# Attention scores of two heads in blocks of 32 queries, four blocks side by side in the PSUM partitions, in one run of TensorE

## The chip, the cores and the metric

The kernel runs on one core of one Trainium2 chip. The metric is the device time of one execution in microseconds (us); the median of several runs counts.

A core has five engines with an instruction queue each: TensorE (matrix multiplies, PE in the profile, its weight loads PEld), VectorE (DVE), ScalarE (ACT), GpSimd (POOL) and SyncE (SP), which here issues every DMA. TensorE writes to PSUM, eight banks of 512 float32 columns in 128 partitions; VectorE and ScalarE read it, GpSimd and DMAs can't.

## What is computed

An attention of two parts feeds a mixing layer and a feed-forward net. `B, H, S, D` are 8, 8, 576 and 64; everything is float32.

```python
q_d, k_d, v_d = means over groups of 4 positions            # 144 positions
out_up = repeat(softmax(scale * q_d @ k_d.T) @ v_d, 4)      # pooled attention
mask = abs(pos[:, None] - pos[None, :]) < 4                 # 7 keys for each query
scores = where(mask, scale * q @ k.T, -1e9)
out_local = softmax(scores) @ v                             # local attention
x = (out_up + out_local)  as (batch, 576, 512)              # heads side by side
h = x.T @ U @ V                                             # mixes positions, rank 32
u = x + h.T
out = u + relu(u @ w_ch1) @ w_ch2                           # 512 -> 2048 -> 512
```

## The kernel before

**Work.** Two heads make a pair (`b`, `hp`), so there are 32. Head 0 of a pair lies in partitions 0 to 63, head 1 in 64 to 127 (`heads`). The first five pairs (`NE`) take another way (`local_blocks`); the other 27, the late pairs, are those of this change. The feed-forward (`ffn1`, `ffn2`) takes 256 steps over 8 batches, two halves of 288 positions and 16 blocks of 128 hidden units; a step is 12 matmuls into `ps_h` and 12 into four banks `acc`. Each weight and each input of it is a pair of a high and a low part in a reduced float32 form (`W1H`, `W1L`, `uH`, `uL`, ...), of which three products are taken.

**A late pair** goes this way:

- SyncE loads `gq` and `gT`, the transposed q and (padded) k of both heads, 128 partitions by 576 and 582. GpSimd makes the pooled `smq` and `smk` of them (L407, L410).
- Dense scores (`qk_group`, L658): 96 queries against the 102 keys around them, six blocks a head; of a block's scores only the band of 7 a query is wanted later. A first run takes four blocks of both heads into two banks (4 x 102 = 408 columns), a second the other two blocks and, behind them in the same banks, the pooled scores (L671, 72 x 144, two a head).
- ScalarE copies the dense scores out of PSUM (`se`, L676), and SyncE writes them to a scratch in HBM, `s_s` (L680), at a row pitch of 103 with rows written at a pitch of 102. So the read back (`sc`, L686) with the pitch of 103 finds the 7 wanted scores of a query at the start of its row.
- The pooled scores go through maximum (DVE L473), exponential (ACT L481), transposes (PE L495) and a second product (PE L506) to `od`, and by HBM (`up_s`) to the local part.
- The local part (`local_attn`): softmax of `sc`, then GpSimd multiplies (L727) and VectorE sums (L732) windows of v; the result goes by HBM (`x_s`) to `mix_part`, which makes `uH` and `uL` for the feed-forward.

**What sets the order.** `Plan` simulates five engines with a duration given for each operation (`op(PE, 1.6, ...)`) and priorities (attention before feed-forward, `FILL`), and writes each engine's instructions in the resulting order. On the chip each engine works its list in that order, and waits on semaphores. The attention of batch b + 1 is spread among the feed-forward steps of batch b. Of the PSUM banks, two (`ps_m`, tag `m`) serve all small work of the late pairs: dense and pooled scores (both banks at once, `psum_pair`), `ps_t`, `ps_a`, `ps_hu` and `ps_u` one each.

Of the kernel before, what the change touches and what calls it, by code (L numbers as in the profile page):

```python
# [11 lines left out]
F32 = mybir.dt.float32  # L12
# [3 lines left out]
AF = mybir.ActivationFunctionType  # L16
# [5 lines left out]
PE, DVE, ACT, POOL, SP = range(5)  # L22
# [31 lines left out]
class Plan:  # L54
# [6 lines left out]
    def buf(self, pool, shape, dt, name, tag=None, bufs=1):  # L61
        return Buf(self, pool, shape, dt, name, tag or name, bufs)

    def op(self, eng, dur, fn, r=(), w=(), prio=0.0, after=(), lat=None, move=0.0, at=0.0):
        o = Op()
        o.eng, o.dur, o.fn, o.prio, o.succ, o.ndep, o.ready = eng, dur, fn, prio, [], 0, at
        o.lat, o.move = LATENCY[eng] + SLACK * (SLACK_FROM <= prio < 1000) if lat is None else lat, move
        deps = set(after)
        bufs = []
        for k in r:  # L70
            b = k[0] if isinstance(k, tuple) else k
            bufs.append(b)
            if k in self.last_w:
                deps.add(self.last_w[k])
            self.readers.setdefault(k, []).append(o)
        for k in w:
            b = k[0] if isinstance(k, tuple) else k
            bufs.append(b)
            if k in self.last_w:
                deps.add(self.last_w[k])  # L80
            deps.update(self.readers.get(k, ()))
            self.readers[k] = []
            self.last_w[k] = o
        deps.discard(o)
        o.margin = MARGIN[eng] * (MARGIN_FROM <= prio < 1000 and any(d.eng != eng for d in deps))
        o.bufs = [b for b in dict.fromkeys(bufs) if isinstance(b, Buf)]
        for b in o.bufs:
            b.uses += 1
        for d in deps:
            d.succ.append(o)  # L90
        o.ndep = len(deps)
        self.ops.append(o)
        return o
# [108 lines left out]
def attn_mix_ffn_kernel(ctx: ExitStack, tc, q, kp, vp, qT, kT, v, U, Ub, V, w1, w2, mask, band, eye, sel, pool, vw, ident, outT):  # L202
    nc = tc.nc
    B, H, S, D = q.shape
# [3 lines left out]
    SD = S // 4  # L208
    QH = SD // 2
# [18 lines left out]
    NB = 6  # L228
    HB = NB // 2
    QB = S // NB  # L230
    KB = band.shape[1] // (HB + 1)

    plan = Plan()
    op, buf = plan.op, plan.buf

    const = ctx.enter_context(tc.tile_pool(name="const", bufs=1))
    loc = ctx.enter_context(tc.tile_pool(name="loc", bufs=1))
# [3 lines left out]
    dram = ctx.enter_context(tc.tile_pool(name="dram", bufs=1, space=bass.MemoryType.DRAM))  # L241
    ps_acc = ctx.enter_context(tc.tile_pool(name="ps_acc", bufs=1, space=bass.MemoryType.PSUM))
    ps_h = ctx.enter_context(tc.tile_pool(name="ps_h", bufs=2, space=bass.MemoryType.PSUM))
    ps_m = ctx.enter_context(tc.tile_pool(name="ps_m", bufs=2, space=bass.MemoryType.PSUM))

    def psum(pool, name, tag, bufs):
        return buf(pool, [128, 512], F32, name, tag, bufs)

    def psum_pair(pool, name, tag, bufs):
        two = [psum(pool, name, tag, bufs) for _ in range(2)]  # L250
        for t in two:
            t.mates = two
        return two

    def dma(fn, r, w, prio, kb=295.0, issue=0.47, lat=1.3):
        late = (3.0 if r else 4.0) * (prio >= 50)
        return op(SP, issue, fn, r, w, prio, move=0.01 + kb / 290.0, at=AT if prio >= 35 else 0.0, lat=lat + late)
# [4 lines left out]
    def act(n, fn, r, w, prio, base=0.143):  # L262
        return op(ACT, n / 1200.0 + base, fn, r, w, prio)
# [127 lines left out]
    def work(is_early, pool, shape, dt, name, tag=None, bufs=1):  # L391
        if is_early:
            return buf(early_pool, shape, dt, name, tag, 2)
        return buf(pool, shape, dt, name, tag, bufs)

    heads = [slice(hh * D, (hh + 1) * D) for hh in range(2)]
    count = {"b": 0}

    def global_attn(b, hp, up_s, prio, qt=None, kt=None, vb=None):
        e = qt is not None  # L400
        h0 = 2 * hp
        sq = work(e, glo, [128, SD], F32, "smq")
        sk = work(e, glo, [128, SD], F32, "smk")
# [9 lines left out]
        if e:  # L413
            qr, kr = qt, kt
        else:
            qr = buf(glo, [128, S], F32, "gq")
            kr = buf(glo, [128, SPAD], F32, "gT")
# [20 lines left out]
        else:  # L438
            vr = [work(e, glo, [QH, 2, 4, D], F32, "vr") for _ in range(2)]
            for hh in range(2):  # L440
                dma(lambda hh=hh: nc.sync.dma_start(
                    out=vr[hh](), in_=v[b, h0 + hh].rearrange("(a p r) d -> p a r d", a=2, r=4)),
# [3 lines left out]
            for hh in range(2):  # L446
                x = vr[hh]
                pool_tt(256, lambda x=x: nc.gpsimd.tensor_tensor(  # L448
                    out=x()[:, :, 0:2, :], in0=x()[:, :, 0:2, :], in1=x()[:, :, 2:4, :], op=ALU.add), [x], [x], prio)
                pool_tt(128, lambda x=x, vs=vss[hh]: nc.gpsimd.tensor_tensor(  # L450
                    out=vs(), in0=x()[:, :, 0, :], in1=x()[:, :, 1, :], op=ALU.add), [x], [vss[hh]], prio)
        view = lambda t, n: t()[:QH, :2 * n].rearrange("p (a k) -> p a k", a=2)
        rs = work(e, glo, [QH, 2, 2], F32, "rs", bufs=2)
        if e:
            ps = psum_pair(ps_m, "ps_s", "m:g", 2)
            scores = lambda t: view(t, SD)

            def s_mm():
                for a in range(2):
                    for hh, o in enumerate(heads):  # L460
                        nc.tensor.matmul(view(ps[hh], SD)[:, a], sq()[o, a * QH:(a + 1) * QH], sk()[o],
                                         start=True, stop=True)
            op(PE, pw(prio) * 1.4, s_mm, [sq, sk], ps, prio)
        else:
            s_s = buf(dram, [2, S, KB + 1], F32, "s_s", bufs=4)
            qk_group(0, NBA, qr, kr, s_s, prio - 0.5)
            ps = qk_group(NBA, NB, qr, kr, s_s, prio - 0.4, sq, sk)
            scores = lambda t: pooled_view(t)
        Es = []
        for hh in range(2):  # L470
            p = ps[hh]
            mx = work(e, glo, [QH, 2], F32, "mx", bufs=2)
            dve(288, lambda p=p, mx=mx: nc.vector.tensor_reduce(  # L473
                out=mx(), in_=scores(p), axis=AX.X, op=ALU.max), [p], [mx], prio)
# [14 lines left out]
        for hh in range(2):  # L489
# [13 lines left out]
            def a_mm(ET=ET, pa=pa, vs=vsx[hh]):  # L503
# [6 lines left out]
                out=od()[:QH, 2 * hh:2 * hh + 2, :], in0=view(pa, D),  # L510
# [141 lines left out]
            w = bass.AP(tensor=a.tensor, offset=a.offset, ap=[[NPOS * D, 64], [1, (NPOS + 6) * D]])  # L652
            nc.sync.dma_start(out=t[hh * 64:(hh + 1) * 64].rearrange("p s d -> p (s d)"), in_=w)

    NBA = 4
    pooled_view = lambda t: t()[:QH, (NB - NBA) * KB:(NB - NBA) * KB + 2 * SD].rearrange("p (a k) -> p a k", a=2)

    def qk_group(n0, n1, qr, kr, s_s, prio, sq=None, sk=None):  # L658
        m = n1 - n0
        view = lambda t: t()[:QB, :m * KB].rearrange("p (i k) -> p i k", i=m)  # L660
        ps = psum_pair(ps_m, "ps_b", "m:b" if sq is None else "m:g", 2)

        def mm():
            for n in range(n0, n1):
                for hh, o in enumerate(heads):
                    nc.tensor.matmul(view(ps[hh])[:, n - n0], qr()[o, n * QB:(n + 1) * QB],  # L666
                                     kr()[o, n * QB:n * QB + KB], start=(n == n0), stop=(n == n1 - 1 and sq is None))
            if sq is not None:
                for a in range(2):
                    for hh, o in enumerate(heads):  # L670
                        nc.tensor.matmul(pooled_view(ps[hh])[:, a], sq()[o, a * QH:(a + 1) * QH], sk()[o],  # L671
                                         start=False, stop=(a == 1))
        op(PE, 0.4 + 0.083 * 2 * m + (0.0 if sq is None else 0.5), mm, [qr, kr] + ([] if sq is None else [sq, sk]), ps, prio)
        for hh in range(2):
            se = buf(loc, [QB, m, KB], F32, f"se{m}", bufs=2)
            act(m * KB, lambda p=ps[hh], se=se: nc.scalar.activation(se(), view(p), AF.Copy), [ps[hh]], [se], prio)  # L676

            def put(hh=hh, se=se):
                dst = s_s()[hh].rearrange("(i p) k -> i (p k)", i=NB)[n0:n1, 0:QB * KB]
                nc.sync.dma_start(out=dst.rearrange("i (p k) -> p i k", k=KB), in_=se())  # L680
            dma(put, [se], [(s_s, n0, hh)], prio, 55 * m)
        return ps

    def local_scores(s_s, prio):
        sc = buf(loc, [128, NPOS, 7], F32, "sc")
        dma(lambda: nc.sync.dma_start(out=sc(), in_=s_s()[:, :, 0:7].rearrange("h (c s) o -> (h c) s o", s=NPOS)),  # L686
            [(s_s, n0, hh) for n0 in (0, NBA) for hh in range(2)], [sc], prio, 315, lat=0.8)
        return sc

    def local_attn(b, hp, up_s, x_s, s_s, prio):  # L690
        h0 = 2 * hp
        lb = lambda shape, name, tag=None, bufs=1: buf(loc, shape, F32, name, tag, bufs)
        vl = lb([128, NPOS + 6, D], "vl")
        sc = local_scores(s_s, prio - 1.5)
        dma(lambda: load_padded(vl(), vp, b, h0), [], [vl], prio + 0.1, 500, 1.2, 2.1)
        ms, mx = lb([128, NPOS, 7], "ms"), lb([128, NPOS], "lmx")
# [203 lines left out]
    for i in range(len(steps) + LAG):  # L900
        if i < len(steps):
            b, t, fc = steps[i]
# [69 lines left out]
```

## Time and profile before

| | |
|---|---|
| median of 3 runs | 1083.02 us (1081.96 to 1083.38) |
| the profiled execution | 1082.04 us |
| its span, first to last instruction | 1080.0 us |
| mean granted clock of TensorE | 0.979 |
| TensorE busy | 1044.0 us (97%) |
| VectorE, ScalarE, GpSimd busy | 537.1, 412.7, 559.2 us |
| late pairs' dense matmuls (L666) | 648 records, 44.1 us |
| late pairs' pooled matmuls (L671) | 216 records, 18.4 us |

A row of a group of instructions names line, engine, operation and tiles (out<-in), partitions x elements, count, then busy time, mean ns of one, and what ended the idle time before it. A row of the timeline has start, length, engine, line, operation and tiles, and how many records it merges. A matmul's row lasts until its modelled end, so neighbouring rows overlap; what counts is the distance from start to start. A wait "<- issue" is time in which nothing was released that the profile shows.

### The profile page before, as it was taken

How to read it: one execution, taken by the hardware profiler on the slowest of the kernel's cores; microseconds unless marked ns; L12 is line 12 of the kernel's file. 1: busy time of each engine (PE TensorE's matmuls, PEld its weight loads, DVE VectorE, ACT ScalarE, POOL GpSimd, SP SyncE). 2: the span in 40 equal slices, each digit the busy share in tenths (PEclk: the TensorE clock that was granted, in tenths of full speed). 3: DMA queues.
4: the chain of work that ended last, by engine and by line, in shares of the span. 5: the costliest groups of instructions: out<-in, count | busy, mean ns of one | idle time of the engine just before them, and what ended most of it. 6: DMA issues, size and time to landing. Idle time of an engine off the chain costs nothing.

```text
span 1080.0 us, 22707 instructions
## 1 busy us (share of the span) xinstructions
PE 1044.0 (97%) x8696; PEld 1012.8 (94%) x8696; DVE 537.1 (50%) x1093; ACT 412.7 (38%) x1374; POOL 559.2 (52%) x580
## 2 busy tenths in 40 slices
PE   7798998998999999999999999999999999999998
PEld 6677897997999999999999999999999999999998
DVE  5888898554554445545454534533466343212111
ACT  4787554343334433333444324422444222211110
POOL 3754567587475756566566726753666614201010
PEclk8897999998999999999999999999999999999999
DMA  6635864555556555554756345642666231000000
GB/s 195 188 118 158 222 195 112 147 121 141 121 142 137 133 147 126 130 137 110 158 139 156 89 97 140 161 104 61 154 148 169 64 71 47 23 1 23 2 22 22
DMA packets 222972, 125.00 MB, mean 116 GB/s; under 512 B 170449, under 2 KB 201491, under 8 KB 222865
## 3 DMA queue, kind: packets, MB, share of 16 engines
q1 hardware_dynamic: 222864, 123.57, 45.5%
q8 instruction: 68, 1.11, 0.4%
q14 instruction: 40, 0.32, 0.1%
HBM read 85.18 MB, written 38.35 MB: 114 GB/s over the span
## 4 chain that ended last, share of the span: by engine, by line
PE 86%; DVE 7%; DMA 2%; ACT 2%; POOL 1%; issue 1%; SPq 0%; DVEq 0%; POOLq 0%; ACTq 0%
PE acc L837 36%; PE ps_h L814 36%; PE ps_b L666 3%; PE ps_a L506 3%; PE ps_hu L774 2%; DVE c L333 1%; DVE c L335 1%; PE ps_t L495 1%; PE ps_b L671 1%; DVE c L328 1%; PE ps_u L789 1%; DMA s_s<-se 1%; DMA xL<-x_s 1%; PE ps_ba L598 1%; DMA kd<-in_kT 0%
## 5 line engine op out<-in xcount | busy, mean ns | idle before, releaser
L837 PE MATMUL acc<-hH,W2H 128*128 128x288 f32 x1024 | 313.2, 306 | 0.0
L814 PE MATMUL ps_h<-uH,W1H 128*128 128x288 f32 x1024 | 307.1, 300 | 0.3 <-ACT ob L608 0.3
L814 PE MATMUL ps_h<-uL,W1H 128*128 128x288 f32 x1024 | 304.8, 298 | 0.0
L814 PE MATMUL ps_h<-uH,W1L 128*128 128x288 f32 x1024 | 304.7, 298 | 0.0
L837 PE MATMUL acc<-hH,W2L 128*128 128x288 f32 x1024 | 302.9, 296 | 0.6 <-POOL W2L L340 0.6
L837 PE MATMUL acc<-hL,W2H 128*128 128x288 f32 x1024 | 303.2, 296 | 0.0
L822 DVE SCALAR_TENSOR_TENSOR hL<-ps_h,hH 128x288 fp32r<-128x288 f32 x256 | 116.6, 456 | 374.8 <-ACT hH L821 373.5
L727 POOL TENSOR_TENSOR Pt<-vl,at 128x896 f32<-128x896 f32 (+1 forms) x135 | 230.9, 1787 | 104.4 <-DVE acc L732 50.6
L821 ACT ACTIVATE hH<-ps_h 128x288 fp32r<-128x288 f32 x256 | 105.0, 410 | 454.3 <-PE ps_h L814 452.8
L837 PEld LDWEIGHTS acc<-hH,W2H 128*128 128x128 f32 x1024 | 193.2, 189 | 6.2 <-issue 3.8
L814 PEld LDWEIGHTS ps_h<-uH,W1H 128*128 128x128 f32 x1024 | 194.2, 190 | 1.9 <-issue 1.2
L814 PEld LDWEIGHTS ps_h<-uL,W1H 128*128 128x128 f32 x1024 | 194.3, 190 | 0.0
L837 PEld LDWEIGHTS acc<-hH,W2L 128*128 128x128 f32 x1024 | 193.2, 189 | 0.8 <-POOL W2L L340 0.8
L814 PEld LDWEIGHTS ps_h<-uH,W1L 128*128 128x128 f32 x1024 | 193.7, 189 | 0.0
L837 PEld LDWEIGHTS acc<-hL,W2H 128*128 128x128 f32 x1024 | 193.5, 189 | 0.0
L732 DVE TENSOR_REDUCE acc<-Pt 128x128 f32<-128x1024 f32 (+1 forms) x135 | 144.8, 1104 | 9.5 <-POOL Pt L727 3.6
L797 POOL TENSOR_TENSOR uL<-xT,uH 128x288 fp32r<-128x288 f32 x56 | 44.0, 807 | 103.4 <-ACT uH L795 103.4
L766 POOL TENSOR_TENSOR xL<-xL,xH 116x640 fp32r<-116x640 f32 x28 | 44.3, 1580 | 82.7 <-ACT xH L765 61.3
L847 POOL TENSOR_TENSOR o<-uH,uL 128x288 f32<-128x288 f32 x64 | 50.1, 814 | 53.3 <-DMA out_t<-o 53.3
L721 ACT ACTIVATE Pt<-ul 128x128 f32<-128x128 f32 (+1 forms) x135 | 48.4, 443 | 24.9 <-DVE acc L732 24.6
L448 POOL TENSOR_TENSOR vr<-vr 72x256 f32<-72x256 f32 x54 | 41.6, 770 | 29.7 <-DMA vr<-in_v 29.5
L676 ACT ACTIVATE se<-ps_b 96x408 f32<-96x408 f32 (+1 forms) x108 | 40.8, 419 | 33.3 <-PE ps_b L666 15.7
(136 smaller groups left out, 1225.3 us busy)
## 6 DMA issues: line engine op xcount, KB each, us to landing
vl<-in_vp SPq DMA_DIRECT2D x54, 240.0 KB
out_t<-o SPq DMA_DIRECT2D x64, 144.0 KB
s_s<-se SPq DMA_DIRECT2D x54, 153.0 KB
w1r<-in_W SPq DMA_DIRECT2D x16, 512.0 KB
w2r<-in_W SPq DMA_DIRECT2D x16, 512.0 KB
Y<-x_s SPq DMA_DIRECT2D x112, 72.0 KB
xL<-x_s SPq DMA_DIRECT2D x28, 287.5 KB
gT<-in_kT SPq DMA_DIRECT2D x27, 291.0 KB
```

Of the source, the lines that this page charges most:

```text
L448: pool_tt(256, lambda x=x: nc.gpsimd.tensor_tensor(out=x()[:, :, 0:2, :], in0=x()[:, :, 0:2, :], in1=x()[:, :, 2:4, :], op=ALU.add), [x], ...
L676: act(m * KB, lambda p=ps[hh], se=se: nc.scalar.activation(se(), view(p), AF.Copy), [ps[hh]], [se], prio)
L721: act(n * D, lambda n=n, ps=ps, Pt=Pt: nc.scalar.activation(Pt()[:, :n, :, 7], ul()[:, ps, :], AF.Copy), [ul], [(Pt, 1)], prio, 0.16)
L727: nc.gpsimd.tensor_tensor(out=Pt()[:, :n, :, 0:7].rearrange("p s d o -> p o s d"), in0=win, in1=at()[:, ps, :].rearrange("p s o -> p o s") ...
L732: dve(8.5 * n * D, lambda n=n, ps=ps, Pt=Pt: nc.vector.tensor_reduce(out=acc()[:, ps, :], in_=Pt()[:, :n], axis=AX.X, op=ALU.add), [(Pt, 0 ...
L766: pool_tt(640, lambda: nc.gpsimd.tensor_tensor(out=xL(), in0=xL().bitcast(F32), in1=xH().bitcast(F32), op=ALU.subtract), [xL, xH], [xL], prio)
L797: pool_tt(TN, lambda uH=uH, uL=uL, uf=uf: nc.gpsimd.tensor_tensor(out=uL()[:, hp, :], in0=uf(), in1=uH()[:, hp, :].bitcast(F32), op=ALU.su ...
L814: nc.tensor.matmul(ps()[:, :TN], w[:, dc, fs], u()[:, dc, :], start=(n == 0), stop=(n == 3 * NDC - 1))
L821: last_h[i] = act(TN, lambda: nc.scalar.activation(hH(), ps()[:, :TN], AF.Relu), [ps], [hH], FIRST, 0.05)
L822: dve(TN, lambda: nc.vector.scalar_tensor_tensor(hL(), ps()[:, :TN], 0.0, hH().bitcast(F32), op0=ALU.max, op1=ALU.subtract), [ps, hH], [hL ...
L837: nc.tensor.matmul(ac[e]()[:, :TN], W2[w][:, fc, es], hx(), start=(fc == 0 and n == 0), stop=(fc == NFC - 1 and n == 2))
L847: pool_tt(TN, lambda e=e, o1=o1: nc.gpsimd.tensor_tensor(out=o1()[:, :TN], in0=uH()[:, e, :].bitcast(F32), in1=uL()[:, e, :].bitcast(F32), ...
```

## The change

Blocks have 32 queries and 38 keys (`QL`, `KL`), 18 a head. Block n goes to row `r = n // 4` and column `c = n % 4`: its 32 queries lie in the PSUM partitions 32c to 32c + 31, and its 38 scores in the columns from 38r on, so that four blocks lie side by side in the partitions and five rows take 190 columns (the fifth row holds two blocks). The pooled scores follow in the same bank, and dense and pooled matmuls are one operation of the plan, with one pair of banks. ScalarE copies four rows of 128 partitions and then the fifth of 64. SyncE writes four transfers a head instead of two, one for each 32 partitions. The scratch has a pitch of 39 instead of 103. Lines between the two places of the diff move up by one, those behind it down by 6: the feed-forward's L814 and L837 become L820 and L843, the dense matmuls L666 become L667.

```diff
-            s_s = buf(dram, [2, S, KB + 1], F32, "s_s", bufs=4)
-            qk_group(0, NBA, qr, kr, s_s, prio - 0.5)
-            ps = qk_group(NBA, NB, qr, kr, s_s, prio - 0.4, sq, sk)
+            s_s = buf(dram, [2, S, KL + 1], F32, "s_s", bufs=4)
+            ps = late_scores(qr, kr, sq, sk, s_s, prio - 0.4)
...
+    QL, KL = 32, 38
+    NL = S // QL
+    NR, NX = divmod(NL, 4)
+    pooled_view = lambda t: t()[:QH, (NR + 1) * KL:(NR + 1) * KL + 2 * SD].rearrange("p (a k) -> p a k", a=2)
+
+    def late_scores(qr, kr, sq, sk, s_s, prio):
+        view = lambda t: t()[:, :(NR + 1) * KL].rearrange("p (r k) -> p r k", r=NR + 1)
+        ps = psum_pair(ps_m, "ps_b", "m:g", 2)
 
         def mm():
-            for n in range(n0, n1):
+            for n in range(NL):
+                r, c = divmod(n, 4)
                 for hh, o in enumerate(heads):
-                    nc.tensor.matmul(view(ps[hh])[:, n - n0], qr()[o, n * QB:(n + 1) * QB],
-                                     kr()[o, n * QB:n * QB + KB], start=(n == n0), stop=(n == n1 - 1 and sq is None))
...
+                    nc.tensor.matmul(view(ps[hh])[c * QL:(c + 1) * QL, r], qr()[o, n * QL:(n + 1) * QL],
+                                     kr()[o, n * QL:n * QL + KL], start=(r == 0), stop=(c == 3 and n + 4 >= NL))
+            for a in range(2):
+                for hh, o in enumerate(heads):
+                    nc.tensor.matmul(pooled_view(ps[hh])[:, a], sq()[o, a * QH:(a + 1) * QH], sk()[o],
+                                     start=False, stop=(a == 1))
+        op(PE, 1.6, mm, [qr, kr, sq, sk], ps, prio)
         for hh in range(2):
-            se = buf(loc, [QB, m, KB], F32, f"se{m}", bufs=2)
-            act(m * KB, lambda p=ps[hh], se=se: nc.scalar.activation(se(), view(p), AF.Copy), [ps[hh]], [se], prio)
+            se = buf(loc, [128, NR + 1, KL], F32, "se", bufs=2)
+            parts = ((0, NR, 128), (NR, NR + 1, NX * QL))
+            for r0, r1, n in parts:
+                act((r1 - r0) * KL, lambda p=ps[hh], se=se, r0=r0, r1=r1, n=n: nc.scalar.activation(
+                    se()[:n, r0:r1], view(p)[:n, r0:r1], AF.Copy), [ps[hh]], [(se, r0)], prio)
 
             def put(hh=hh, se=se):
-                dst = s_s()[hh].rearrange("(i p) k -> i (p k)", i=NB)[n0:n1, 0:QB * KB]
-                nc.sync.dma_start(out=dst.rearrange("i (p k) -> p i k", k=KB), in_=se())
-            dma(put, [se], [(s_s, n0, hh)], prio, 55 * m)
+                for c in range(4):
+                    to = s_s()[hh, c * QL:(c + 1) * QL, :]
+                    n = NR + (c < NX)
+                    dst = bass.AP(tensor=to.tensor, offset=to.offset, ap=[[KL, QL], [4 * QL * (KL + 1), n], [1, KL]])
+                    nc.sync.dma_start(out=dst, in_=se()[c * QL:(c + 1) * QL, 0:n])
+            dma(put, [(se, 0), (se, NR)], [(s_s, hh)], prio, 100, 1.7)
```

The fourth late pair on TensorE, before: its first run (`ps_b` are the dense scores, `acc` and `ps_h` the feed-forward).

```order
L837 MATMUL acc_1554<-hL,W2H 128x288
L837 MATMUL acc_1554<-hH,W2L 128x288
L666 MATMUL ps_b<-gT,gq 96x102 x8
L837 MATMUL acc_1561<-hH,W2H 128x288
```

Its second run, some 20 rows later, with the pooled scores (`smk`, `smq`):

```order
L814 MATMUL ps_h<-uL,W1H 128x288
L814 MATMUL ps_h<-uH,W1L 128x288
L666 MATMUL ps_b<-gT,gq 96x102 x4
L671 MATMUL ps_b<-smk,smq 72x144 x4
L837 MATMUL acc_1554<-hH,W2H 128x288
```

And the same pair's only run now:

```order
L820 MATMUL ps_h<-uL,W1H 128x288
L820 MATMUL ps_h<-uH,W1L 128x288
L667 MATMUL ps_b<-gT,gq 32x38 x36
L671 MATMUL ps_b<-smk,smq 72x144 x4
L843 MATMUL acc_1615<-hH,W2H 128x288
```

The feed-forward is interrupted in one place instead of two, for 36 small dense matmuls instead of 8 and 4 larger ones; the four pooled ones stay.

SyncE's list around the same pair's scores, before (`gq`, `gT` are loads for the next pair, `ul` and `sc` reads from HBM for the local part):

```order
L680 DMA s_s<-se_2260 96x4x102
L680 DMA s_s<-se_2277 96x4x102
L526 DMA gq<-in_qT 128x576
L526 DMA gT<-in_kT 128x582
L680 DMA s_s<-se_2307 96x2x102
L680 DMA s_s<-se_2316 96x2x102
L715 DMA ul<-up_s 128x576
L686 DMA sc<-s_s 128x9x7
```

and now:

```order
L525 DMA gq<-in_qT 128x576
L525 DMA gT<-in_kT 128x582
L686 DMA s_s<-se 32x5x38 x2
L686 DMA s_s<-se 32x4x38 x2
L686 DMA s_s<-se 32x5x38 x2
L686 DMA s_s<-se 32x4x38 x2
L692 DMA sc<-s_s 128x9x7
```

Eight transfers of 32 partitions stand where two of four blocks and two of two blocks stood, all behind the loads for the next pair, and the read `sc` follows them at once.

More of the change, by code (lines that the diff above doesn't have):

```diff
@@ L653, in load_padded @@
             nc.sync.dma_start(out=t[hh * 64:(hh + 1) * 64].rearrange("p s d -> p (s d)"), in_=w)
[L655 to L661, printed above, removed]
+    QL, KL = 32, 38
+    NL = S // QL
@@ L668, in mm @@
[L668 to L673, printed above, removed]
-        for hh in range(2):
-            se = buf(loc, [QB, m, KB], F32, f"se{m}", bufs=2)
-            act(m * KB, lambda p=ps[hh], se=se: nc.scalar.activation(se(), view(p), AF.Copy), [ps[hh]], [se], prio)
-            def put(hh=hh, se=se):
-                dst = s_s()[hh].rearrange("(i p) k -> i (p k)", i=NB)[n0:n1, 0:QB * KB]
-                nc.sync.dma_start(out=dst.rearrange("i (p k) -> p i k", k=KB), in_=se())
-            dma(put, [se], [(s_s, n0, hh)], prio, 55 * m)
+                    nc.tensor.matmul(view(ps[hh])[c * QL:(c + 1) * QL, r], qr()[o, n * QL:(n + 1) * QL],
+                                     kr()[o, n * QL:n * QL + KL], start=(r == 0), stop=(c == 3 and n + 4 >= NL))
@@ L686, in local_scores @@
         dma(lambda: nc.sync.dma_start(out=sc(), in_=s_s()[:, :, 0:7].rearrange("h (c s) o -> (h c) s o", s=NPOS)),
-            [(s_s, n0, hh) for n0 in (0, NBA) for hh in range(2)], [sc], prio, 315, lat=0.8)
+            [(s_s, hh) for hh in range(2)], [sc], prio, 315, lat=0.8)
         return sc
```

## The prediction

> **What bounds the kernel now.** I read the page first (busy shares and the chain that ended last), then a table by stretch, then the chain and the waits of TensorE from 265 us on, and last the rows of TensorE around two runs of dense scores. From the page:
>
> ```profile
> span 1080.0 us, 22707 instructions
> PE 1044.0 (97%) x8696; PEld 1012.8 (94%) x8696; DVE 537.1 (50%) x1093; ACT 412.7 (38%) x1374; POOL 559.2 (52%) x580
> PE 86%; DVE 7%; DMA 2%; ACT 2%; POOL 1%; issue 1%; SPq 0%; DVEq 0%; POOLq 0%; ACTq 0%
> ```
>
> Matmuls are pipelined, so 97% says only that TensorE is the first suspect; that 86% of the chain is its work says more. By stretch (busy time of PE, PEld, DVE, ACT, POOL; granted clock; DMA share; GB/s):
>
> ```profile
> 0.00:100.00 100.00, 80.69 (x696) 69.26 (x696) 78.77 (x157) 71.53 (x292) 56.24 (x70) 0.88 0.56 161
> 100.00:200.00 100.00, 92.06 (x742) 87.41 (x743) 81.13 (x148) 51.56 (x150) 62.30 (x61) 0.93 0.68 177
> 200.00:300.00 100.00, 94.79 (x791) 92.64 (x791) 52.97 (x98) 37.29 (x120) 65.03 (x62) 0.97 0.53 126
> 300.00:400.00 100.00, 100.00 (x879) 97.30 (x876) 47.59 (x107) 40.87 (x138) 65.30 (x71) 1.00 0.60 146
> ```
>
> From 300 us on TensorE has no hole and the full clock; before 200 us VectorE, at 81%, shares the bound. The chain of 265 to 1080 us and what TensorE's loads wait for there:
>
> ```profile
> by line: PE acc L837 44.6%; PE ps_h L814 43.3%; PE ps_b L666 3.6%; PE ps_a L506 2.8%; PE ps_hu L774 1.8%; PE ps_t L495 1.3%; PE ps_b L671 1.3%; PE ps_u L789 0.8%; DVE o L850 0.2%; issue 0.0%; DVEq L850 0.0%
> ```
> ```profile
> PEld ps_b L666 <- issue: 6.1, 37, 0.2
> PEld acc L837 <- issue: 3.1, 16, 0.2
> PEld ps_h L814 <- issue: 1.0, 5, 0.2
> PEld ps_b L666 <- DVE at L710: 0.3, 2, 0.2
> ```
>
> So in this stretch nobody is waited for: whatever TensorE is given less of, the end moves by that much. The only holes stand at the dense runs themselves: 37 times about 0.16 us as TensorE enters one, with nothing released at that moment, and again as it leaves.
>
> **Price of the two runs today.** One pair's first run, with the feed-forward matmuls around it, and its second run:
>
> ```profile
> 299.20 0.30 PE L814 MATMUL ps_h<-uL,W1H 128*128 128x288 f32 x1
> 299.33 0.29 PE L814 MATMUL ps_h<-uH,W1L 128*128 128x288 f32 x1
> 299.56 0.95 PE L666 MATMUL ps_b<-gT,gq 64*96 64x102 f32 x16
> 300.44 0.40 PE L837 MATMUL acc<-hH,W2H 128*128 128x288 f32 x1
> 300.68 0.30 PE L837 MATMUL acc<-hL,W2H 128*128 128x288 f32 x1
> ```
> ```profile
> 308.25 0.29 PE L814 MATMUL ps_h<-uH,W1L 128*128 128x288 f32 x1
> 308.47 0.60 PE L666 MATMUL ps_b<-gT,gq 64*96 64x102 f32 x8
> 308.90 0.66 PE L671 MATMUL ps_b<-smk,smq 64*72 64x144 f32 x8
> 309.49 0.40 PE L837 MATMUL acc<-hH,W2H 128*128 128x288 f32 x1
> 309.73 0.29 PE L837 MATMUL acc<-hL,W2H 128*128 128x288 f32 x1
> ```
> ```profile
> L666 PE MATMUL ps_b<-gT,gq x648: 245/248/481, 93.9 to 876.2; 64*96 64x102 f32 x162
> L671 PE MATMUL ps_b<-smk,smq x216: 281/282/441, 101.8 to 876.6; 64*72 64x144 f32 x108
> ```
>
> A feed-forward matmul starts every 0.13 us (299.20 to 299.33). From the last one before a run to the second one after it takes 300.68 - 299.33 = 1.35 and 309.73 - 308.25 = 1.48 us; less two such steps (0.27) the runs cost 1.08 and 1.21, together **2.29 us a pair**. What they are made of: 648 records for 27 x 12 matmuls, so a float32 matmul is two loads and two multiplies. A multiply lasts 0.248 us, so in the run of 16 the last one starts 0.95 - 0.248 = 0.70 us after the first, in the run of 8 after 0.35: eight more in 0.35, or 0.088 us for every two. The pooled ones: (0.66 - 0.282) / 3 = 0.126 for every two. The step grows by 0.038 over 42 columns, 0.9 ns a column, and hardly anything is fixed; 38 columns then take about 0.035 us. That it is two at a time, one of each head, shows in a window on the run's beginning, which counts one multiply and one load in its first 0.01 us and two of each in 0.02:
>
> ```profile
> 308.46:308.47 0.01, 0.00 (x1) 0.00 (x1) 1.00 0.34 128
> 308.46:308.48 0.02, 0.01 (x2) 0.01 (x2) 1.00 0.17 64
> ```
>
> The two heads' tiles, in the two halves of the array's rows, run beside each other. The loads, first of the run and third:
>
> ```profile
> 299.56 0.78 PEld L666 LDWEIGHTS ps_b<-gT,gq 64*96 64x96 f32 x16 [0.17 <-issue]
> ```
> ```profile
> 299.64 0.25 PEld L666 LDWEIGHTS ps_b<-gT,gq 64*96 64x96 f32 x4
> ```
>
> 0.08 us for 96 columns of one half, so about 0.027 for 32. The switches: into the run 308.25 to 308.47 is 0.22 instead of 0.13. Out of it, the last pooled multiply starts at 308.90 + 0.38 = 309.28 and streams 0.12; the next load comes at 309.49, 0.09 later; then two steps of the feed-forward take 0.24 instead of 0.13, while 128 columns are loaded uncovered. Between dense and pooled today there is no pause beyond the ordinary step.
>
> **The change, part by part.** TensorE has one run a pair instead of two: 36 dense matmuls (72 loads, 72 multiplies, 38 columns, eight tiles of 64 x 32), then the same pooled ones. With D for the dense part: 0.22 in + 0.03 first load + D + change of tile 0.15 + pooled 0.50 + out 0.09 + 0.24 - 0.27 = **0.96 + D**. The change of tile inside the run is bounded by 0 (96 to 72 columns today) and by a switch as at the ends (0.09 + 0.06 to load 72 columns); I take the upper end, since the tile's width does change.
>
> No row of before shows tiles beside each other in the columns, so D has bounds. Below: five rounds of eight tiles, two records each, 10 x 0.035 = 0.35. With the two heads beside each other as now and the columns one after the other: 36 x 0.035 = 1.26. If the columns do overlap, but each half works its list in order, the second record of a block waits 0.035 for the first and the next block's first starts right behind it: 18 x 0.04 = 0.72; 72 records that start at most 0.01 apart, as the two heads' do, give at most 0.72 too. I take 0.65: halves that run their lists side by side are the nearest thing the rows show. The run is then 1.61, and a pair saves 2.29 - 1.61 = 0.68 us.
>
> The Trainium skill (TensorE: Matmul & The Clock Gate, Measured speedup vs the span model) states 2.38 times for three column tiles at 512 columns; no run here shows it. By that rate for four, 1.26 would become about 0.40, an estimate from that page, and a pair would save 0.93.
>
> How many pairs count: 27 have such runs. The pooled matmuls of before 200 us, and the dense ones of before 265 us:
>
> ```profile
> L671 PE MATMUL ps_b<-smk,smq x32: 282/283/441, 101.8 to 173.2; 64*72 64x144 f32 x32
> ```
> ```profile
> L666 PE MATMUL ps_b<-gT,gq x144: 245/248/481, 93.9 to 254.3; 64*96 64x102 f32 x144
> ```
>
> At 8 and 24 records a pair these are four and six pairs. Up to 200 us VectorE is as much the bound (81% against 92%), so I count the four there half: 25 x 0.68 = 17.0 us.
>
> The rest costs nothing by itself. ScalarE evicts 152 and 38 columns a head instead of 408 and 204:
>
> ```profile
> L676 ACT ACTIVATE se<-ps_b 96x408 f32<-96x408 f32 x54 | 25.3, 504 | 15.7 <-PE ps_b L666 15.7
> L676 ACT ACTIVATE se<-ps_b 96x204 f32<-96x204 f32 x54 | 15.5, 334 | 17.6 <-PE ps_b L671 15.4 <-DVE mx L473 2.2
> ```
>
> At 0.83 ns a column that is 0.29 + 0.20 instead of 0.84 us; its 38% covers either. One bank pair is taken a pair instead of two, so the feed-forward is interrupted once. The dense scores now also wait for the pooled q and k from GpSimd; the pooled matmuls, which wait for them today at nearly the same place, show no idle time. SyncE issues eight transfers of scores instead of four, in front of the read `sc` and of the loads queued behind:
>
> ```profile
> L680 SPq DMA_DIRECT2D s_s<-se x108: 304/395/1597, 99.0 to 878.2; - x108
> ```
>
> Four more at 0.30 to 0.40 us put every later issue back by 1.2 to 1.6 us. After 265 us nothing of TensorE waits for that. Before, the chain does pass it:
>
> ```profile
> 126.04 6.19 DMA s_s<-se
> ```
> ```profile
> 236.02 5.70 DMA xL<-x_s
> ```
>
> Six pairs lie there; all of it on the chain would cost 6 x 1.6 = 10 us, and scores that come in one run instead of two may as well come sooner. I take 0 and keep 10 for the range. Sum: 1080.0 span, 1082.04 with what lies around it; 1082.0 - 17.0 = 1065.0. The profiled run is 1.0 below the median 1083.02, so **1066**.
>
> **The rivals.** (1) Columns overlap freely: D = 0.4, saves 0.93 x 25 = 23: 1060. Nothing in the rows speaks against it but that eight tiles are more than two. (2) Loads of one half go one after the other, as 0.08 us for 96 columns suggests: 36 x 0.029 = 1.04, saves 0.29 x 25 = 7: 1076. (3) The change doesn't do what it says: columns run one after the other, D = 1.26, saves 0.07 x 25 = 2: 1081. The streamed columns then grow from 6 x 102 = 612 to 18 x 38 = 684 a head, and only the saved switch pays for it. (4) Slower: TensorE's issue becomes the limit. The dense part has 144 instructions instead of 48. Before never shows a long run denser than the dense ones, 8 loads and 8 multiplies in 0.35 us, 44 ns a load and multiply; at that rate D = 3.17, a pair costs 4.13, and 25 x 1.84 = 46 us are lost: 1129. It decides from D = 1.33 on, 18.5 ns a load and multiply. Against it: 44 ns there is the streaming of two times 102 columns, and two of each start within 0.02 us.
>
> The Trainium skill (the same page, Wait — 56ns, not 53.3ns?) has a rule that speaks for (4): starts of matmuls never come closer than about 25 ns, however few columns. By it D = 72 x 0.025 = 1.80, an estimate, and the time 1083 + 12 = 1095. The trace doesn't agree where two halves are concerned (two starts in 0.02 us at most); for column tiles it shows nothing.
>
> **How the numbers follow.** Chances: forecast 0.40, (1) 0.13, (2) 0.16, (3) 0.11, (4) 0.15, lateness of scores before 265 us eating the gain 0.05. The range from 1055 (case 1 with the holes before 265 us smaller) to 1092 leaves out (4) and a little below; the forecast's own is 1060 to 1073. Within 0.2% (2 us, about what these runs can tell from no change) falls half of (3): same 0.08, faster 0.72, slower 0.20.
>
> **What would show it.** One run of the dense line a pair with 1944 multiplies in all; from the feed-forward matmul before it to the second one behind it 1.9 us (1.61 + 0.27) in the stretch after 265 us, 1.7 for (1), 2.3 for (2), 2.5 for (3), over 2.6 for (4). A hole of 0.1 to 0.15 us between dense and pooled. TensorE without waits after 300 us, as now. The prediction is wrong if the run is longer than 2.3 us, or if new waits of TensorE on GpSimd or transfers appear before 300 us.

## The result and the profile after

The changed kernel takes 1065.98 us (median of 4 runs, 1062.85 to 1066.61) where the kernel before, beside it, takes 1083.2 (1081.96 to 1083.82): ratio 0.9837, interval 0.9815 to 0.9858, 17.2 us saved. The profiled execution is the fastest of the four, 1062.85 us; its page begins:

```profile
span 1061.1 us, 25383 instructions
PE 1019.2 (96%) x9992; PEld 991.7 (93%) x9992; DVE 545.2 (51%) x1093; ACT 391.1 (37%) x1374; POOL 562.9 (53%) x580
PE 74%; POOL 3%; DVE 2%; issue 1%; DMA 1%; ACT 1%; SPq 0%; ACTq 0%; POOLq 0%; DVEq 0%
```

TensorE has 1296 multiplies more (9992 against 8696) and is busy 24.8 us less; it is still the bound. The 74% of the last row are a share of the span, and the chain of this page goes back only to 182 us: of what it covers TensorE's work is 90%, and from 265 us on 95%, where it was 99% before. One pair's run in the timeline of TensorE (start, length, line, tiles, records merged):

```profile
514.81 0.29 PE L843 MATMUL acc<-hL,W2H 128*128 128x288 f32 x1
514.94 0.30 PE L843 MATMUL acc<-hH,W2L 128*128 128x288 f32 x1
515.17 0.85 PE L667 MATMUL ps_b<-gT,gq 64*32 64x38 f32 x72
515.95 0.71 PE L671 MATMUL ps_b<-smk,smq 64*72 64x144 f32 x8
516.59 0.40 PE L820 MATMUL ps_h<-uH,W1H 128*128 128x288 f32 x1
516.83 0.30 PE L820 MATMUL ps_h<-uL,W1H 128*128 128x288 f32 x1
```

From the feed-forward matmul before the run to the second one behind it 516.83 - 514.94 = 1.89 us; less 0.27, the run costs **1.62 us**, and 18 of the 21 runs after 265 us cost 1.615 to 1.63, where a pair's two runs cost 2.29 before. The line's group, and the dense line's own multiplies and loads in a narrow window at the run's beginning:

```profile
L667 PE MATMUL ps_b<-gT,gq x1944: 191/202/268, 94.2 to 858.2; 64*32 64x38 f32 x195
```
```profile
515.16:515.35 0.19, 0.18 (x32) 0.18 (x33) 1.00 0.07 24
```

A multiply is 0.20 us long, so the last of the 72 starts 0.85 - 0.20 = 0.65 us after the first. They aren't evenly spaced: 32 of them start in the first 0.18 us, and about as many loads (the counts in the window's brackets); the other 40 take the remaining 0.47.

Stretches from 200 us on (busy time of PE, PEld, DVE, ACT, POOL; clock; DMA share; GB/s), the chain from 265 us on, and the longest waits of TensorE's loads after 290 us that are for another engine (total, times, longest):

```profile
200.00:300.00 100.00, 97.56 (x994) 95.73 (x994) 55.93 (x108) 37.52 (x127) 73.68 (x70) 1.00 0.54 130
300.00:400.00 100.00, 100.00 (x1018) 98.68 (x1017) 50.07 (x104) 36.29 (x125) 61.13 (x65) 1.00 0.50 118
...
600.00:700.00 100.00, 98.72 (x1079) 96.65 (x1078) 49.65 (x104) 37.02 (x137) 60.93 (x62) 1.00 0.50 124
700.00:800.00 100.00, 99.65 (x1007) 98.18 (x1005) 49.57 (x104) 33.67 (x121) 57.86 (x63) 1.00 0.46 111
```
```profile
by line: PE acc L843 43.0%; PE ps_h L820 42.3%; PE ps_a L505 2.7%; PE ps_b L667 1.9%; PE ps_hu L780 1.8%; PE ps_b L671 1.5%; PE ps_t L494 1.4%; DVE acc L738 0.9%; DMA xL<-x_s 0.8%; PE ps_u L795 0.7%; DMA x_s<-acc 0.3%; issue 0.2%; DVE mx L4
```
```profile
PEld ps_t L494 <- ACT E L480: 1.3, 2, 0.7
PEld ps_hu L780 <- POOL xL L772: 0.9, 1, 0.9
```

In the first two stretches TensorE is as full as before or fuller; between 600 and 800 us it has holes of 1.6 us. New are the two rows of waits, and with them `DVE acc` and `DMA xL<-x_s` in the chain: TensorE is nearer to running out of other work. One of the waits, 0.9 us for `xL` at 649.7 us, hangs on SyncE: the chain passes four transfers of scores from 638.94 to 640.60 us, and the load `xL` behind them. The 256 feed-forward steps are the same in both kernels, so their start times tell where the gain falls (us, the profiled execution of each):

```
step            40     120     152     200     255
before       283.9   597.0   718.1   896.3  1073.1
after        278.9   580.5   701.7   877.1  1054.2
difference    -5.0   -16.5   -16.4   -19.2   -18.9
```

From step 40 to 200, 20 pairs: the intervals that hold the dense runs went from 46.9 to 33.1 us, the steps between feed-forward matmuls from 502.9 to 500.9 (20 fewer ways out of a run at 0.11 us), all other interruptions from 62.7 to 64.2. That is about the size of the holes, but there are also 113 of these interruptions where there were 103, and the two weren't told apart. Together -14.2.

The -5.0 of step 40 is less sure than the rest. Two more profiled executions of the changed kernel start step 40 at 277.9 and 280.5 us, and the granted clock up to 200 us differs between executions (from 0 to 100 and 100 to 200 us 0.90 and 0.97 after, 0.88 and 0.93 before). From step 40 to 255 the three agree within 0.6 us.

### The profile page after: what moved, and what is told of

It reads as the page before. It is cut to its first block, busy times and chain, and to the rows that moved or that the text cites. A ratio compares the mean times of both kernels' runs of the same rounds, so it can differ in the third digit from the quotient of the medians.

```text
span 1061.1 us, 25383 instructions
## 1 busy us (share of the span) xinstructions
PE 1019.2 (96%) x9992; PEld 991.7 (93%) x9992; DVE 545.2 (51%) x1093; ACT 391.1 (37%) x1374; POOL 562.9 (53%) x580
## 4 chain that ended last, share of the span: by engine, by line
PE 74%; POOL 3%; DVE 2%; issue 1%; DMA 1%; ACT 1%; SPq 0%; ACTq 0%; POOLq 0%; DVEq 0%
PE acc L843 33%; PE ps_h L820 33%; PE ps_a L505 2%; PE ps_b L667 1%; POOL Pt L733 1%; PE ps_hu L780 1%; PE ps_b L671 1%; PE ps_t L494 1%; DVE acc L738 1%; PE ps_u L795 1%; DMA xL<-x_s 1%; POOL xL L772 1%; POOL uL L803 0%; DVE ms L704 0%; DVE o L856 0%
## 5 line engine op out<-in xcount | busy, mean ns | idle before, releaser
L843 PE MATMUL acc<-hH,W2H 128*128 128x288 f32 x1024 | 312.0, 305 | 0.0
L820 PE MATMUL ps_h<-uH,W1H 128*128 128x288 f32 x1024 | 306.3, 299 | 0.1
L820 PE MATMUL ps_h<-uH,W1L 128*128 128x288 f32 x1024 | 303.2, 296 | 0.0
L843 PE MATMUL acc<-hL,W2H 128*128 128x288 f32 x1024 | 303.0, 296 | 0.0
L843 PE MATMUL acc<-hH,W2L 128*128 128x288 f32 x1024 | 302.2, 295 | 0.5 <-POOL W2L L340 0.5
L820 PE MATMUL ps_h<-uL,W1H 128*128 128x288 f32 x1024 | 300.5, 293 | 0.0
L733 POOL TENSOR_TENSOR Pt<-vl,at 128x896 f32<-128x896 f32 (+1 forms) x135 | 231.9, 1802 | 107.4 <-DVE acc L738 64.2
L843 PEld LDWEIGHTS acc<-hH,W2H 128*128 128x128 f32 x1024 | 193.1, 189 | 3.1 <-issue 3.1
L820 PEld LDWEIGHTS ps_h<-uH,W1H 128*128 128x128 f32 x1024 | 193.1, 189 | 2.4 <-issue 2.1
L820 PEld LDWEIGHTS ps_h<-uL,W1H 128*128 128x128 f32 x1024 | 194.3, 190 | 0.0
L843 PEld LDWEIGHTS acc<-hH,W2L 128*128 128x128 f32 x1024 | 192.9, 188 | 0.7 <-POOL W2L L340 0.7
L843 PEld LDWEIGHTS acc<-hL,W2H 128*128 128x128 f32 x1024 | 193.3, 189 | 0.0
L820 PEld LDWEIGHTS ps_h<-uH,W1L 128*128 128x128 f32 x1024 | 193.3, 189 | 0.0
L505 PE MATMUL ps_a<-vs,E 72*72 72x64 f32 x432 | 36.6, 227 | 3.5 <-ACT E L498 3.0
```

The source lines that it names most:

```text
L505: nc.tensor.matmul(view(pa, D)[:, a, :], ET()[:, c, a * QH:(a + 1) * QH], vs()[:, c, :], start=(c == 0), stop=(c == 1))
L733: nc.gpsimd.tensor_tensor(out=Pt()[:, :n, :, 0:7].rearrange("p s d o -> p o s d"), in0=win, in1=at()[:, ps, :].rearrange("p s o -> p o s") ...
L820: nc.tensor.matmul(ps()[:, :TN], w[:, dc, fs], u()[:, dc, :], start=(n == 0), stop=(n == 3 * NDC - 1))
L843: nc.tensor.matmul(ac[e]()[:, :TN], W2[w][:, fc, es], hx(), start=(fc == 0 and n == 0), stop=(fc == NFC - 1 and n == 2))
```

## The experiments

Four theories. A, the forecast's: each half of the array's rows works its list in order, the columns overlap only as far as that. B: columns overlap freely, and the rate at which TensorE gets instructions sets the dense part. C: columns don't overlap. D: the time in which SyncE writes the scores counts after all. Each kernel is the changed one with one edit. For the price of a run, read from its timeline as above, one place is shown; medians are over the runs after 265 us.

### The changed kernel again

> The changed kernel as it is, beside the others on the same chip. Both theories: 1066 us, within 3, and 1.62 us a run after 265 us (from the last feed-forward matmul before it to the second one behind it, less two steps).

1061.34 us (1061.14 to 1066.19), ratio 0.9809 (0.9783 to 0.9835), run 1.62 us. Executions of this kernel spread from 1061 to 1067 us; edits worth 1 to 3 us are therefore judged by the run's price in the trace.

### The list column by column

> Same 36 dense matmuls, same places in PSUM, but listed column by column: the five blocks of PSUM partitions 0 to 31 first, then those of 32 to 63, and so on, so that neighbours in the list share a tile. Theory A (column tiles overlap, each half of the rows works in list order): every record now waits 0.035 us for the one before it in its tile, 36 x 0.035 = 1.26 us instead of 0.65 for the dense part, 2.2 us a run, 25 x 0.6 = 15 us more, 1081 us. Theory B (column tiles overlap freely, the dense part lasts 0.65 us because instructions don't come faster): 1.26 too if TensorE only overlaps neighbours, under 0.9 us if it picks any tile out of its queue, 1066 to 1081. Rival C (tiles in the columns don't overlap and the gain is elsewhere): no change, 1066.

```diff
-            for n in range(NL):
-                r, c = divmod(n, 4)
+            for c, r in [(c, r) for c in range(4) for r in range(NR + (c < NX))]:
+                n = 4 * r + c
```

1070.06 us (1069.65 to 1072.31), ratio 0.988 (0.9852 to 0.9909). Its timeline:

```profile
520.25 0.30 PE L843 MATMUL acc<-hH,W2L 128*128 128x288 f32 x1
520.47 1.13 PE L667 MATMUL ps_b<-gT,gq 64*32 64x38 f32 x72
521.53 0.71 PE L671 MATMUL ps_b<-smk,smq 64*72 64x144 f32 x8
522.17 0.40 PE L820 MATMUL ps_h<-uH,W1H 128*128 128x288 f32 x1
522.41 0.29 PE L820 MATMUL ps_h<-uL,W1H 128*128 128x288 f32 x1
```

Dense 1.13 - 0.20 = 0.93 us instead of 0.65, run 522.41 - 520.25 - 0.27 = 1.89. The same 72 multiplies cost 0.28 us more when neighbours in the list share a tile. So the columns do overlap in the changed kernel, against C, and the order of the list matters. A (1.26 us, 1081) missed; B had 1.26 or under 0.9, and 0.93 lies near its second case. In the column's own order the step is mostly 0.033 us for one multiply of each head, as 38 columns one at a time would have it.

### Half the keys

> Each dense matmul streams 19 of its 38 keys; the other half of the scores is left out (ScalarE copies the 19 twice, so everything behind stays as large). Theory A (waits of the second record for the first, 0.035 us of streaming): the step halves to about 0.018, the dense part falls from 0.65 to about 0.35 us, 25 x 0.3 = 7.5 us less, 1058 us. Theory B (supply of instructions): the dense part stays at 0.6 to 0.65 us, 1064 to 1067 us.

```diff
-                    nc.tensor.matmul(view(ps[hh])[c * QL:(c + 1) * QL, r], qr()[o, n * QL:(n + 1) * QL],
-                                     kr()[o, n * QL:n * QL + KL], start=(r == 0), stop=(c == 3 and n + 4 >= NL))
+                    nc.tensor.matmul(view(ps[hh])[c * QL:(c + 1) * QL, r, 0:19], qr()[o, n * QL:(n + 1) * QL],
+                                     kr()[o, n * QL:n * QL + 19], start=(r == 0), stop=(c == 3 and n + 4 >= NL))
```

It computes 19 of a block's 38 scores and copies them twice. 1063.87 us (1060.98 to 1066.82), ratio 0.9818 (0.979 to 0.9847).

```profile
516.39 0.30 PE L845 MATMUL acc<-hH,W2L 128*128 128x288 f32 x1
516.62 0.80 PE L667 MATMUL ps_b<-gT,gq 64*32 64x19 f32 x72
517.35 0.71 PE L671 MATMUL ps_b<-smk,smq 64*72 64x144 f32 x8
517.99 0.40 PE L822 MATMUL ps_h<-uH,W1H 128*128 128x288 f32 x1
518.23 0.30 PE L822 MATMUL ps_h<-uL,W1H 128*128 128x288 f32 x1
```

Half the columns, yet the run is 1.57 us, 0.05 less; dense is 0.62 us, as a multiply is 0.18 long here. If streaming had set the dense part, as A has it, it would have halved. A falls; the streaming isn't what takes 0.65 us. The time agrees: A had it 7.5 us below the changed kernel's, and it lies within that kernel's spread.

### The dense multiplies in two runs

> The small blocks side by side, but in two runs with a bank pair each, as before: eight blocks a head (32 multiplies) in the first, ten and the pooled scores in the second; the transfers stay 8. Theory B (supply): the first run's 32 multiplies start within 0.2 us, the second's 40 within 0.4; the way into and out of a second run costs about 0.33 us, so the two runs together cost 1.85 to 1.95 us against 1.62, 25 x 0.28 = 7 us more: 1068 to 1072. Theory A: 8 x 0.04 = 0.32 us for the first run's multiplies, 1.95 us together and more. Rival (one run is what gained): 2.29 us as before, 1080 or more.

The first 8 blocks (32 multiplies) run in a bank pair of their own and the other 10 with the pooled scores:

```diff
+        pa = run(0, RA, "m:b", False, 0.55)
...
+        ps = run(RA, NR + 1, "m:g", True, 1.35)
```

1071.74 us (1071.24 to 1075.0), ratio 0.9909 (0.9883 to 0.9935). Both runs:

```profile
531.88 0.29 PE L834 MATMUL ps_h<-uH,W1L 128*128 128x288 f32 x1
532.10 0.37 PE L671 MATMUL ps_b<-gT,gq 64*32 64x38 f32 x32
532.40 0.40 PE L857 MATMUL acc<-hH,W2H 128*128 128x288 f32 x1
532.64 0.29 PE L857 MATMUL acc<-hL,W2H 128*128 128x288 f32 x1
...
533.96 0.29 PE L857 MATMUL acc<-hH,W2L 128*128 128x288 f32 x1
534.18 0.58 PE L671 MATMUL ps_b<-gT,gq 64*32 64x38 f32 x40
534.69 0.71 PE L677 MATMUL ps_b<-smk,smq 64*72 64x144 f32 x8
535.33 0.40 PE L834 MATMUL ps_h<-uH,W1H 128*128 128x288 f32 x1
535.57 0.30 PE L834 MATMUL ps_h<-uL,W1H 128*128 128x288 f32 x1
```

32 multiplies start in 0.37 - 0.20 = 0.17 us and their run costs 532.64 - 531.88 - 0.27 = 0.49; the second costs 1.34. Together 1.83 (medians 0.50 + 1.35) against 1.62: the dense multiplies by themselves became quicker, 0.17 + 0.38 instead of 0.65, but a second way in and out costs 0.33. One run is worth 0.23 us a pair in this price, and the time lies in the range of B, but not for this reason. From step 40 to 200 this kernel takes 598.6 us and the changed one 598.2 in the profile above: its dense runs cost 4.3 us more there, and its other interruptions, 103 instead of 113 in the other order that the plan gives it, 4.0 us less. It is slower before step 40, which starts at 290.6 us instead of 277.9 to 280.5 (this profiled execution is the slowest of its four); why wasn't taken apart. So in the stretch after step 40 nearly all of the gain over the kernel before, which takes 612.4 us there, comes from the small tiles side by side, and the merging of the runs adds nothing that shows. B's rate holds: after a stretch of feed-forward work the first 32 are always quick, whichever 32 they are.

### Where the pooled scores stand

> In the one run the pooled matmuls come before the dense ones. Theory B in the form that TensorE works off what is queued (64 instructions, of which 32 multiplies of dense scores started within 0.18 us) and then waits for more: the pooled ones take 0.5 us, in which instructions behind them can be fetched; if the hole of 0.1 us after the 32nd multiply is the start of fetching, it goes and a run costs 1.5 us, 2 to 3 us less (1059 to 1063); if fetching only starts again when the queue has nearly run dry, the hole moves to another place and nothing changes (1062 to 1066).

With the pooled multiplies ahead of the dense ones: 1065.97 us (1063.28 to 1068.43), ratio 0.9848 (0.9815 to 0.9881), no difference in time. The pause behind the 32nd dense multiply stands in all 21 runs after 265 us. Thirteen of them cost 1.62 us; the other eight cost 1.70 to 1.81, with a second pause of 0.06 to 0.17 us behind 59 to 63 dense multiplies.

> The eight pooled multiplies stand between the first 32 and the last 40 dense ones. In the trace of the changed kernel the first 32 dense starts take 0.18 us, then there is a hole of 0.1 us, and the other 40 come at 9 ns each. Theory B (the first 32 were already waiting at TensorE, the others arrive at the pace at which instructions are supplied): while the pooled multiplies stream for 0.5 us the supply catches up, 32 of the last 40 start within 0.2 us, the other 8 at 9 ns; the dense part shrinks from 0.65 to about 0.45 us, a second change of tile costs 0.1 to 0.15 us; run 1.48 to 1.58 us against 1.62, the time 1 to 3 us below the changed kernel's. Theory X (the 40 are slow because of what they do in the array: drain of the columns, writes to one bank): they stay at 9 ns each, the second change of tile is added; run 1.72 to 1.80 us, the time 2 to 4 us above the changed kernel's.

```diff
+            dense(range(16))
             for a in range(2):
...
+            dense(range(16, NL))
```

1066.38 us (1065.31 to 1067.26), ratio 0.9849 (0.9835 to 0.9863). A block leaves four records, two a head, so 16 blocks are 64 multiplies and not 32: the split stood too far back to test B. The run costs 1.754 us, 0.13 more, which is the price of a second change of tile inside a run. The split behind 8 blocks:

> As e8, with the split where e8 should have had it: a block's multiply leaves two records a head, so the first 32 records are 8 of the 18 blocks, and e8 split behind 64 records. There the run cost 1.754 us against 1.62, so a second change of tile costs 0.13. Now 32 dense records, the eight pooled, 40 dense. Theory B (the first 32 were waiting at TensorE, the others come as they are supplied): the second part's first 32 start within 0.18 to 0.2 us, then a hole of about 0.07 and some 8 at 9 ns, dense streams 0.18 + 0.28 in place of 0.65, run 1.754 - 0.19 = 1.56 us (1.50 to 1.62), the time 1 to 3 us below e8, about that of the changed kernel. Theory X (the later records are slow because of the array): the 40 at 9 ns each, run 1.72 to 1.78, the time as e8.

1067.3 us (1064.14 to 1068.61), ratio 0.9859 (0.9834 to 0.9883). Its timeline, and a window on the beginning of the second dense part:

```profile
520.11 0.30 PE L846 MATMUL acc<-hH,W2L 128*128 128x288 f32 x1
520.33 0.37 PE L668 MATMUL ps_b<-gT,gq 64*32 64x38 f32 x32
520.63 0.71 PE L673 MATMUL ps_b<-smk,smq 64*72 64x144 f32 x8
521.27 0.57 PE L668 MATMUL ps_b<-gT,gq 64*32 64x38 f32 x40
521.78 0.40 PE L823 MATMUL ps_h<-uH,W1H 128*128 128x288 f32 x1
522.02 0.30 PE L823 MATMUL ps_h<-uL,W1H 128*128 128x288 f32 x1
```
```profile
521.27:521.46 0.19, 0.18 (x32) 1.00 0.30 69
```

The multiplies from the 33rd on, slow in the changed kernel, now follow 0.6 us of pooled work, and 32 of them start within 0.19 us, as B had it; the last 8 take the other 0.19 of 0.57 - 0.20. Dense is 0.17 + 0.37 = 0.54 us instead of 0.65. Against e8 the run falls from 1.754 to 1.648; B said 1.56, since it made the last 8 quicker than they are. X, by which the run stays at 1.72 or more, falls, though the run lies outside B's range too. The second change of tile eats the gain, and the times of the two don't differ.

### More and fewer transfers

> The scores go out in 16 transfers a pair of 16 partitions each instead of 8 of 32; the plan's order is the same. Theory A and B both hold SyncE off the path after 265 us: the same runs and steps there, 1066 us within 3. Rival D (SyncE's issues cost time): 8 more at 0.43 us are 3.4 us a pair; where the chain passes the scores, before 265 us, 6 pairs x 3.4 = up to 20 us more.

```diff
+                    for g in range(2):
+                        h = QL // 2
...
+                        nc.sync.dma_start(out=dst, in_=se()[c * QL + g * h:c * QL + (g + 1) * h, 0:n])
```

The bytes stay, but each of the eight transfers of a pair is cut into two of 16 partitions. 1098.47 us (1096.83 to 1100.39), ratio 1.0136 (1.0114 to 1.0159): 37 us above the changed kernel on the same chip, with the run still at 1.62. The group of these transfers (min/median/max ns) in the changed kernel, and then here; what TensorE waits for after 290 us here; a stretch of it; the chain from 265 us on; and a stretch of SyncE's queue:

```profile
L686 SPq DMA_DIRECT2D s_s<-se x216: 302/430/1727, 99.5 to 863.4; - x108
```
```profile
L689 SPq DMA_DIRECT2D s_s<-se x432: 302/425/1672, 100.8 to 903.0; - x144
```
```profile
PEld ps_hu L783 <- POOL xL L775: 9.8, 9, 1.3
PEld ps_hu L783 <- ACT xH L774: 7.7, 5, 5.3
PEld ps_t L494 <- ACT E L480: 2.6, 1, 2.6
```
```profile
600.00:700.00 100.00, 93.01 (x935) 91.02 (x934) 44.78 (x91) 32.52 (x116) 51.39 (x53) 0.97 0.43 105
```
```profile
by line: PE acc L846 33.8%; PE ps_h L823 32.2%; SPq L689 7.5%; DMA xL<-x_s 5.9%; PE ps_b L667 1.9%; PE ps_a L505 1.9%; issue 1.7%; POOL xL L775 1.7%; PE ps_b L671 1.5%; PE ps_hu L783 1.5%; DVE acc L741 1.2%; DVE mx L472 0.7%; ACT xH L774 0.
```
```profile
663.94 4.18 SPq L689 DMA_DIRECT2D s_s<-se  x9
668.17 0.33 SPq L759 DMA_DIRECT2D xL<-x_s  x1
668.54 0.60 SPq L761 DMA_DIRECT2D xL<-x_s  x1
```

Half the size, and the transfer keeps its 0.43 us on SyncE: the cost is by the transfer. The other engines' lists have the same order as in the changed kernel, so the transfers are all that differs. Nine of them take 4.18 us, and the load `xL` that the later stage needs stands right behind. TensorE then waits for that stage (`ps_hu` for `xL` and `xH`), and SyncE's time on these transfers is 7.5% of the stretch, where the chain of before has none of it and that of after 1.5 us. The DMA engines, 43% busy, aren't the limit, and SyncE isn't full either: of the 560 us from 300 to 860 its issues take 333 in the changed kernel and 398 here. What counts is what stands in its list behind a group of transfers. D holds at sixteen.

> The scores of both heads go out together, in 4 transfers a pair of twice the size instead of 8, and are read back in 2 instead of 1: 3 issues of SyncE less a pair, though bigger ones. TensorE's runs unchanged, 1.62 us. Theory D (SyncE's time counts: twice the transfers, 3.6 us a pair more, cost some 33 us): 1 to 1.5 us a pair less on SyncE gives 3 to 8 us, 1055 to 1062. Rival (it counts only when SyncE is nearly full): 1061 to 1066, no change.

```diff
-                    dst = bass.AP(tensor=to.tensor, offset=to.offset, ap=[[KL, QL], [4 * QL * (KL + 1), n], [1, KL]])
-                    nc.sync.dma_start(out=dst, in_=se()[c * QL:(c + 1) * QL, 0:n])
+                dst = bass.AP(tensor=to.tensor, offset=to.offset,
+                              ap=[[KL, QL], [4 * QL * (KL + 1), 2 * (NR + 1)], [1, KL]])
+                nc.sync.dma_start(out=dst, in_=se()[c * QL:(c + 1) * QL].rearrange("p h r k -> p (h r) k"))
```

Both heads' scores lie in one tile and go in one transfer for each 32 partitions: four writes, and two reads `sc` for one, so six transfers a pair instead of nine. 1060.0 us (1058.85 to 1062.85), ratio 0.9798 (0.9772 to 0.9824). Once more, beside the changed kernel:

> The version with six transfers for a late pair instead of nine, beside the changed kernel on the same chip. Theory D (SyncE's time was on the path a little even with nine): 3 to 7 us below the changed kernel, most of it gained before 400 us and in the small waits between 640 and 790 us. If nine transfers were hidden: within 2 us of it.

> The changed kernel itself as the yardstick of the other three on this chip: 1061 to 1067 us, run 1.62 us.

1058.13 us (1057.93 to 1060.04), ratio 0.9779 (0.9764 to 0.9793), against 1064.71 (1064.4 to 1067.16), ratio 0.9844 (0.9828 to 0.9859). The intervals don't meet: **6.6 us faster than the changed kernel**, the best version here. All 14 executions of the changed kernel have a median of 1064.6 us and the eight of this version 1059.2, 5.4 us less. The run stays at 1.62 us. The profiled executions of the two, 4.4 us apart, differ by 3.3 us at step 48, 2.5 at step 120 and 4.6 at the last step. The 3.3 can't be told from the spread, as the changed kernel's own profiles differ by 2.6 at step 48; the 2.1 after step 120 come where the holes were, which are gone:

```profile
600.00:700.00 100.00, 100.00 (x1093) 98.20 (x1092) 50.51 (x106) 37.99 (x140) 57.35 (x60) 1.00 0.53 125
```

So D is likely at nine transfers too, but small, and not shown: the edit also changes the buffers of `se`, the read `sc` and the durations given to the plan, which puts TensorE's list in another order from 155 us on. None of these was tried apart.

> Both edits, six transfers and pooled between the dense multiplies. If B and D hold: the sum of both, 1054 to 1059 us. If only D: 1058 to 1064. If neither: 1066 or more.

With e8's split on top: 1062.39 us (1060.76 to 1064.93), ratio 0.9816 (0.9798 to 0.9834), 4.3 above e9 and in the range of "only D"; the second change of tile alone makes 27 x 0.13 = 3.5.

## Why the prediction came out as it did

**The price today, 2.29 us a pair, and the run, 1.61.** Right: 1.62, so 0.67 saved where 0.68 was forecast. 27 x 0.67 = 18.1 us is what the runs can give; 17.0 was forecast, 17.2 measured.

**D = 0.65.** The value was right by luck, the reason wrong. "Each half works its list in order, 18 x 0.04" would have halved at 19 keys; it lost 0.03 (e3). What the runs showed in its place is two rates: 32 multiplies at 0.0055 us each, then 40 at 0.012 with the pause between. By the first rate alone D would be 72 x 0.0055 = 0.40, rival (1). The second begins at the 33rd multiply in every order in which neighbours fall on different tiles (column by column, in e2, the first 32 are no quicker than the rest), and starts anew after 0.6 us of other work (e5, e12). That TensorE holds 32 loads and 32 multiplies ahead and gets the rest as they are supplied fits all of it, but is argued and not shown: what supplies them was not looked at, and a store behind the array that takes 32 results at once and empties more slowly would look the same here.

**Rivals (2), (3), (4).** (2) needed loads one after the other within a half, 0.029 us each; 33 passed in 0.19. (3) needs a price of 2.5 us over the same way where 1.89 stands; part of its serial order came back when the list was put in the column's order (e2). (4) was near in kind and far in size: the rate of instructions, if that is what it is, is the limit from the 33rd on, at 0.012 us a load and multiply, not 0.044, and break-even stood at 0.0185. The Trainium skill's rule (TensorE: Matmul & The Clock Gate, Wait — 56ns, not 53.3ns?) that starts come no closer than 25 ns doesn't hold across tiles here: 32 in 0.18 us. The 2.38 times of the Trainium skill (TensorE: Matmul & The Clock Gate, Measured speedup vs the span model) gave the estimate D = 0.40; the overlap was there, but only the first 32 went at that rate, and D was 0.65.

**Change of tile 0.15.** 515.17 + 0.65 = 515.82 is the last dense start, 515.95 the first pooled load; a further change costs 0.13 (e8).

**SyncE's four more transfers, taken at 0.** This step failed, within the 10 us kept for the range. That TensorE waited for none of them before said only that none was late yet: one of the new waits, 0.9 us, has them in front of it, and eight more cost 37 us (e4). With three issues fewer than the changed kernel has, 6.6 us come back (e9), though not surely for that reason. The sum held all the same, and that was luck: the pairs before 265 us, four of which were counted half, brought -5.0 at step 40 in the profiled execution where 4 x 0.68 = 2.7 was due, which makes up for the 1.6 us of holes, and part of the 5.0 may be the clock's. That e9's 24.4 us below the kernel before exceed the 18.1 that the runs can give means that six transfers, or the buffers or the order that go with them, bring something that the kernel before didn't have either; which, stays open.

**"TensorE without waits after 300 us."** Not quite: its loads wait 2.2 us for `E` and `xL`. The wait of the merged run for the pooled q and k, taken at nothing, shows as 3.0 us in two places, both before 120 us:

```profile
  POOL smk L410: 3.0, 2
```

The pooled matmuls of before had no such wait. New waits of TensorE on GpSimd before 300 us were the prediction's own sign of being wrong; the sign came, at a price too small to upset the forecast.

Open stays how much of the spread of 1061 to 1067 us of one kernel lies before 265 us, where the clock is granted differently from run to run.

## What to carry to other kernels

Cut short matmuls to what is needed and lay them side by side in the columns, in an order in which neighbours in the list fall on different tiles; then, at 38 columns as at 19, the number of multiplies sets the time: 0.0055 us each for the first 32 of a run and 0.012 for those behind. A way into and out of a run costs 0.33 us, a change of tile inside it 0.13; but see in the whole whether merging runs pays, as here ten more interruptions of other kinds took back what it gave. Count the transfers that such a layout adds, at 0.43 us each on their queue, and look at what is queued behind them: a queue that no wait names may still be what the next wait hangs on, and doubling the suspect shows it.

## What was not expected of the hardware

32 multiplies of 64 x 32 tiles start in 0.18 us with 38 columns and 0.16 with 19; the next 40 take 0.47 and 0.46. Neighbours on one tile cost 0.28 us in 72. A transfer from 16 partitions holds SyncE as long as one from 32, 0.43 us, and one of both heads' scores (e9) 0.46.
